# Gate-up products of two blocks as 84 rounds on the two halves of the TensorE array, followed by their eight sums and the steps of attention, with five PSUM banks in a ring

## The chip, the cores and the metric

The kernel runs on one core of one Trainium2 chip. A core has TensorE (PE in the profile, with its weight loads as PEld), VectorE (DVE), ScalarE (ACT), GpSimd (POOL) and SyncE (SP, which here only starts DMAs). The metric is the device time of one execution in microseconds.

## The reference

Input `x` is 2048 tokens of 448 features. It is normalised, and the result feeds two branches whose sum is added to `x`.

```python
xn = _layernorm(x)
# branch A: 16 heads of 28, four segments of 512 tokens, one after the other
q, k, v = heads(xn @ wq), heads(xn @ wk), heads(xn @ wv)
p = softmax(q_s @ k_s.T * scale + causal_mask)          # within segment s
o = g * (phi(q_s) @ M) / (phi(q_s) @ z + 1e-6) + (1 - g) * (p @ v_s)
M, z = M + phi(k_s).T @ v_s, z + sum(phi(k_s))
A = o @ wo
# branch B: a gated unit, 1792 wide
B = (sigmoid(xn @ w_gate) * (xn @ w_up)) @ w_down
return x + A + B
```

## The kernel before

**Numbers.** A wide product is made of fp32r parts: each operand is a high part plus a low part, and high·high, high·low and low·high are summed in PSUM. The 448 features lie in four chunks of the 128 partitions. Three chunks are full; chunk 3 holds the last 64 features twice: rows 0 to 63 hold the high part of `xn`, rows 64 to 127 its low part, and the weights stand there twice. So a product over all features takes 3×3+2 = 11 instructions (`TERMS`, line 53). The last of them, `(3, 7)`, also adds low·low in rows 64 to 127. `xs[b]` holds `xn` transposed, seven chunks for each of four blocks `b` of 512 tokens; `wgu[f]` holds chunks 0 to 7 of the gate and up weights for 128 of the 1792 columns, `f` from 0 to 13.

**The gated branch** (`gated`, line 166) takes `f` in pairs (`f0`, step `FG` = 2) and within each pair the four blocks. A block has four outputs of 128×512 (gate and up for two `f`), each of 11 products into one bank `pgu` (line 247): 44 instructions. When both outputs of an `f` stand, line 255 takes a Tanh of the gate's (`sg`, ACT), line 256 multiplies by the up's (DVE), line 258 copies the high part of `hh` (ACT) and line 259 makes the low part (DVE). A block then has four sums `down` (line 168), one for 128 tokens each: six products of `hh` with `wdn` (line 173) and an addition into `acc` (DVE, line 174). Lines 180 to 203 load the weights by SP and split them on ACT and DVE (lines 85 and 86).

**Attention** (`Pair`, `Unit`, from line 583) works on 32 pairs of heads and segments. A pair's scores are five banks `st` (line 612); each is copied to `w` by ACT (lines 616, 619), masked by POOL (line 627), and reduced for maxima by DVE (lines 629, 633). `weights` (line 639) combines the maxima with DVE and POOL in turn (lines 643 to 653), spreads them (`mb`, line 656), and in three parts subtracts them (DVE, line 666) and takes the exponential (ACT, line 667). Two pairs make a unit, whose product with `v` is `pa` (line 687), and which DVE finishes (lines 690, 136, 693). `attention` (line 700) hands these out in steps, 234 in all.

**What sets the order.** PE and SP run in the order in which the code is written (`MANUAL`, line 55). The loop at line 788 takes one place of the gated branch after another (each `yield`) and issues attention's steps in proportion, about 0.44 of a step to a place. A block has 20 places: three after each output and two after each sum, a sum following each output. Over the main part, ACT, DVE and POOL are put in an order by a scheduler when the kernel is built, and each of them then runs its own list strictly in that order. PSUM has eight banks, in `banks`, line 113: `gu` 2, `p` 2, `pd` 1, and for attention `s` 2 (for `st`) and `m` 1 (for `pa`).

## Time and profile before

| | us |
|---|---|
| median of the two runs shown | 689.47 (689.45 and 689.49) |
| the profiled execution | 689.46 |
| its span | 687.7 |

Of the span, PE is busy 681.7 us, DVE 567.4, ACT 342.6 and POOL 151.3. In the views a group of instructions is given as line, engine, operation, output<-input, shapes and count, then busy time in us and mean ns of one, then the idle time of the engine just before them with what ended it. In a table of windows each engine's busy time stands with the number of instructions. An instruction's own duration includes latency that the next one overlaps, so the spacing of a run of equal instructions is shorter than the mean of one.

### The profile page before, as it was taken

Reading aid. Unit: us, or ns where it says so; the run is one execution under the profiler, and the core shown is the slowest. Engines: PE = TensorE matmul, PEld = TensorE weight load, DVE = VectorE, ACT = ScalarE, POOL = GpSimd, SP = SyncE. Lnnn points to the kernel's source line nnn. Section 1 sums busy time; section 2 is a strip of 40 time slices with the busy share of each in tenths; the row PEclk is TensorE's granted clock in tenths of the full one; section 3 lists DMA queues with packets and bytes.
Section 4 is the critical chain, followed back from the end, with each engine's and each line's share of the span. In section 5 each row is a group of like instructions: output and inputs, shape, how many; then the busy total and the mean of one; then the engine's idle time right before and its main releaser. Section 6 shows DMA issues by size and latency. Waiting matters only on the chain.

```text
span 687.7 us, 10438 instructions
## 1 busy us (share of the span) xinstructions
PE 681.7 (99%) x3594; PEld 566.6 (82%) x3594; DVE 567.4 (83%) x994; ACT 342.6 (50%) x563; POOL 151.3 (22%) x349
## 2 busy tenths in 40 slices
PE   8999999999999999999999999999999999999997
PEld 7898888778878787787878878787787878878897
DVE  6765795767788988998898989989898899889863
ACT  4837555343554555543655446454653565446320
POOL 3500020101223222232332222322322322222000
PEclk9999999999999999999999999999999999999999
DMA  7446556696233323243223252314333332423342
GB/s 267 181 150 238 198 214 242 249 330 174 71 94 92 80 86 86 56 128 112 56 64 107 57 141 56 109 47 116 82 94 77 96 71 64 95 79 95 95 153 106
DMA packets 45796, 84.37 MB, mean 123 GB/s; under 512 B 6320, under 2 KB 20400, under 8 KB 45232
## 3 DMA queue, kind: packets, MB, share of 16 engines
q1 hardware_dynamic: 42736, 76.37, 35.8%
q0 software_dynamic: 3008, 7.34, 4.9%
q8 instruction: 28, 0.46, 0.3%
q14 instruction: 24, 0.20, 0.1%
HBM read 51.05 MB, written 32.64 MB: 122 GB/s over the span
## 4 chain that ended last, share of the span: by engine, by line
PE 70%; DVE 14%; issue 9%; POOL 4%; DMA 1%; ACT 1%; SPq 0%; POOLq 0%; ACTq 0%
PE pgu L247 26%; PE pd L173 13%; PE pp L355 10%; PE po L771 5%; PE pv L335 5%; PE st L612 3%; PE pa L687 3%; DVE mx L629 3%; DVE w L666 2%; POOL w L627 2%; DVE acc L174 2%; PE pmm L383 2%; PE n L401 2%; DVE hh L259 1%; DVE mx L633 1%
## 5 line engine op out<-in xcount | busy, mean ns | idle before, releaser
L247 PE MATMUL pgu<-xs,wgu 128*128 128x512 f32 x1232 | 304.1, 394 | 0.0
L247 PEld LDWEIGHTS pgu<-xs,wgu 128*128 128x128 f32 x1232 | 228.2, 188 | 47.4 <-issue 2.2
L173 PE MATMUL pd<-wdn,hh 128*128 128x448 f32 x672 | 156.0, 367 | 0.0
L627 POOL TENSOR_SCALAR_AFFINE_SELECT w<-w 128x256 f32<-128x256 f32 (+1 forms) x160 | 81.2, 509 | 236.4 <-ACT w L616 183.6
L173 PEld LDWEIGHTS pd<-wdn,hh 128*128 128x128 f32 x672 | 122.5, 188 | 12.3 <-issue 0.6
L667 ACT ACTIVATE w<-w 128x1024 f32<-128x1024 f32 (+1 forms) x96 | 87.3, 915 | 65.0 <-DVE w L666 64.2
L666 DVE TENSOR_TENSOR w<-w,mb 128x1024 f32<-128x1024 f32 (+1 forms) x96 | 98.9, 1045 | 0.1
L616 ACT ACTIVATE w<-st 128x512 f32<-128x512 f32 x128 | 74.9, 590 | 45.3 <-PE st L612 44.9
L629 DVE TRANSPOSE_TENSOR_REDUCE mx<-w 128x32 f32<-128x1024 f32 x64 | 79.0, 1235 | 17.0 <-POOL w L627 17.0
L355 PE MATMUL pp<-xs,wqk 128*128 128x512 f32 x308 | 77.7, 401 | 0.0
L174 DVE TENSOR_TENSOR acc<-pd,acc 128x448 f32<-128x448 f32 x112 | 67.1, 599 | 1.2 <-PE pd L173 1.1
L355 PEld LDWEIGHTS pp<-xs,wqk 128*128 128x128 f32 x308 | 56.8, 188 | 13.4 <-issue 2.4
L258 ACT ACTIVATE hh<-sg 128x512 fp32r<-128x512 f32 x56 | 35.2, 628 | 56.4 <-DVE sg L256 49.3
L612 PE MATMUL st<-qk 84*128 84x128 f32 (+3 forms) x256 | 61.9, 312 | 0.0
L255 ACT ACTIVATE sg<-pgu 128x512 f32<-128x512 f32 x56 | 33.2, 594 | 49.4 <-PE pgu L247 49.2
L612 PEld LDWEIGHTS st<-qk 84*128 84x128 f32 x256 | 47.6, 189 | 6.9 <-ACT w L616 0.3
L656 DVE STREAM_TRANSPOSE mb<-top 128x1024 f32<-128x1024 f32 x32 | 39.8, 1242 | 10.5 <-POOL top L653 10.1
L362 DVE TENSOR_TENSOR qk<-pp,qk 128x512 fp32r<-128x512 f32 x28 | 19.3, 688 | 29.8 <-ACT e L360 23.7
L259 DVE SCALAR_TENSOR_TENSOR hh<-sg,hh 128x512 fp32r<-128x512 f32 x56 | 38.7, 691 | 2.6 <-ACT hh L258 2.4
L335 PE MATMUL pv<-wv,xs 128*128 128x448 f32 x176 | 39.6, 376 | 0.4 <-DVE xs L102 0.3
L687 PE MATMUL pa<-w,vv 128*32 128x128 f32 (+3 forms) x512 | 39.7, 436 | 0.2
L256 DVE SCALAR_TENSOR_TENSOR sg<-sg,pgu 128x512 f32<-128x512 f32 x56 | 37.3, 665 | 1.8 <-PE pgu L247 1.6
(100 smaller groups left out, 640.6 us busy)
## 6 DMA issues: line engine op xcount, KB each, us to landing
qk<-qd SPq DMA_DIRECT2D x192, 112.0 KB
qd<-qk SPq DMA_DIRECT2D x28, 512.0 KB
raw<-in_w_ffn SPq DMA_DIRECT2D x14, 512.0 KB
vd<-vst SPq DMA_DIRECT2D x4, 1024.0 KB
vv<-vd SPq DMA_DIRECT2D x16, 256.0 KB
od<-w POOLq DMA_DIRECT2D x16, 256.0 KB, 3.8
sums<-od SPq DMA_DIRECT2D x32, 128.0 KB
out<-acc SPq DMA_DIRECT2D x16, 224.0 KB
```

The costliest lines, as they stand in the source:

```text
L173: T.matmul(pd[:, :D], l, r, start=n == 0, stop=n == len(mms) - 1)
L174: V.tensor_add(acc[b][:, t, :], pd[:, :D], acc[b][:, t, :])
L247: T.matmul(dst, wgu[f][:, w, side * P:(side + 1) * P], xs[b][:, a, :], start=n == 0, stop=n == len(TERMS) - 1)
L335: T.matmul(pv[:, :D], xs[b][:, a, t * P:(t + 1) * P], wv[w], start=n == 0, stop=n == len(TERMS) - 1)
L355: T.matmul(pp, wqk[c][:, w, :], xs[b][:, a, :], start=n == 0, stop=n == len(TERMS) - 1)
L612: T.matmul(st[:, at:at + L - kb * P], self.qk[:KS, 1, h, kb * P:(kb + 1) * P], self.qk[:KS, 0, h, kb * P:], start=True, stop=True)
L616: A.activation(w, st, AF.Copy)
L627: G.affine_select(d, d, pattern=pattern, base=0, channel_multiplier=-1, compare_op=ALU.is_ge, fill=MASK)
L629: V.tensor_reduce(mx[:, 16 * (n - 1):16 * (n + 1)], w3[:, n // 2, :2 * L].rearrange("p (b n) -> p b n", n=32), axis=mybir.AxisListType.X, ...
L666: V.tensor_sub(w, w, m)
L667: A.activation(w, w, AF.Exp, scale=SCALE)
L687: T.matmul(pa[32 * j:32 * j + 32, kb * P:], self.vv[:, kb, 32 * j:32 * j + 32], self.pairs[j // 2].block(j % 2, kb), start=kb == 0, stop=k ...
```

## The change

A block's 44 products of 128 rows become 42 *rounds*. A round is two products of 64 rows that stand next to each other, one on rows 0 to 63 of the array, the other on rows 64 to 127, into two different banks: the gate's and the up's of one `f`. `PHASES` lists four phases of a block, the first and second `f` with the halves one way round (11 rounds each), then both again turned (10 rounds each), so that each bank gets both halves of every term. The term that was `(3, 7)` is now taken over the 64 rows of the high part alone, once for each output; `xd` is a second copy of that part in the other half of the partitions (made by POOL, once for each block), and which half of chunk 3 holds the low part now depends on `b`.

The four phases of a block have no places in them, so no step of attention is issued there. After the first two phases stands one *mark* each: ACT copies a single element of `xs[b]` onto itself, chunk 6 after the first phase, chunk 5 after the second. It can run when the phase's products with that chunk are done, and later products with that chunk wait for it. These are the tenth round of the second phase (the 42nd of the block's 84 instructions, then the third phase) and, for the second mark, the tenth round of the third phase (the 63rd instruction, then the fourth phase).

Two blocks (`WINDOW`) run one after the other in this way, 84 rounds; then come their eight sums, each now followed by five places, and attention's steps among them. The five banks `gu`, `p`, `gu`, `p`, `pd` are taken in turn for outputs and sums. `raw`, into which the gate-up weights are loaded, has one buffer instead of two. The very first block keeps its 128-row products (`whole`).

```diff
+WINDOW = 2
+PHASES = ([None, (3, 3), (0, 0), (0, 4), (4, 0), (1, 1), (1, 5), (5, 1), (2, 2), (2, 6), (6, 2)],
...
+          [(5, 1), (1, 1), (1, 5), (0, 0), (0, 4), (4, 0), (3, 3), (2, 2), (2, 6), (6, 2)])
...
+    def high_tail(b, side):
+        r = slice(64 * side, 64 * side + 64)
+        return xs[b][r, 3, :] if side == b % 2 else xd[b // 2][r, :]
...
+        def place(n):
+            return ("gu", "p", "gu", "p", "pd")[(ring[0] + n) % 5]
...
-            pd = bank("pd", tag)
+            pd = bank("pd", tag or place(0))
...
-            yield
-            yield
+            for _ in range(places):
+                yield
...
-            raw_up[f] = mid.tile([P, 1024], F32, name="raw", bufs=2)
+            raw_up[f] = mid.tile([P, 1024], F32, name="raw", bufs=1)
...
+        def halves(f0, b, ahead, hs):
+
+            pgu = {}
+            for k, terms in enumerate(PHASES):
+                f, turned = f0 + k % 2, k // 2
+                if not turned:
+                    pgu[f] = [opened(k) for _ in range(2)]
+                for n, term in enumerate(terms):
+                    for h in (1, 0) if turned else (0, 1):
+                        side, r = h ^ turned, slice(64 * h, 64 * h + 64)
+                        a, w = term or (3, 7)
+                        T.matmul(pgu[f][side], wgu[f][r, w, side * P:(side + 1) * P],
+                                 xs[b][r, a, :] if term else high_tail(b, side),
+                                 start=n == 0 and not turned, stop=n == len(terms) - 1 and bool(turned))
+                if not turned:
+
+                    mark = xs[b][64:65, 6 - k, 0:1]
+                    A.activation(mark, mark.bitcast(F32), AF.Copy)
+                else:
+                    hs.append(finish(pgu[f], f))
...
+            ahead[0, 2] = lambda: load_up(f0 + 2)
+            ahead[1, 3] = lambda: load_up(f0 + 3)
...
+                    halves(f0, b, ahead, hs)
+                pending.append(downs(f0, b, hs))
+                if f0 + b > 0 and (b + 1) % WINDOW == 0:
+                    while len(pending) > (1 if WINDOW == 1 or f0 + FG == NF and b == NB - 1 else 0):
+                        for part in pending.pop(0):
+                            yield from part
...
+            high = slice(64, P) if b % 2 else slice(0, 64)
+            G.tensor_copy(xd[b // 2][low_rows(b), :], xs[b][high, 3, :])
```

**PE**, from where the gated branch leaves the first block (`xs_65`) for the second (`xs_66`). Before:

```order
L247 MATMUL pgu<-xs_66,wgu 128x512 x22
L612 MATMUL st<-qk_1642 128x512
L247 MATMUL pgu<-xs_66,wgu 128x512 x11
L612 MATMUL st<-qk_1642 128x384
L612 MATMUL st<-qk_1642 128x128
L173 MATMUL pd<-wdn,hh 128x448 x6
L612 MATMUL st<-qk_1642 128x512
L247 MATMUL pgu<-xs_66,wgu 128x512 x11
L173 MATMUL pd<-wdn,hh 128x448 x6
```

Now, where line 277 is the half-row product, line 193 the sum and line 671 the score:

```order
L277 MATMUL pgu<-xd_73,wgu 128x512
L277 MATMUL pgu<-xs_66,wgu 128x512 x21
L277 MATMUL pgu<-xd_73,wgu 128x512
L277 MATMUL pgu<-xs_66,wgu 128x512 x61
L193 MATMUL pd<-wdn,hh 128x448 x18
L671 MATMUL st<-qk_1645 128x512
L193 MATMUL pd<-wdn,hh 128x448 x6
L671 MATMUL st<-qk_1645 128x384
L671 MATMUL st<-qk_1645 128x128
L193 MATMUL pd<-wdn,hh 128x448 x6
```

Outputs, sums and scores alternated; now all 84 half-row products of this block stand together and the scores come among the sums behind them.

**ACT**, in the third block of the second pair of `f`. Before, with line 667 the exponential, 255 the Tanh, 258 the copy to `hh`, and 616 and 619 the copies of scores:

```order
L255 ACTIVATE sg<-pgu 128x512
L616 ACTIVATE w<-st 128x512
L667 ACTIVATE w<-w 128x2x512
L667 ACTIVATE w<-w 128x2x2x256
L667 ACTIVATE w<-w 128x2x2x128
L258 ACTIVATE hh<-sg 128x512
L616 ACTIVATE w<-st 128x512
L619 ACTIVATE w<-st 128x2x256
L255 ACTIVATE sg<-pgu 128x512
```

Now, with line 283 the mark, 726 the exponential, 236 the Tanh, 239 the copy to `hh`, 675 the copy of a score and 100 a split of weights:

```order
L675 ACTIVATE w<-st 128x512 x3
L283 ACTIVATE xs_67<-xs_67 1x1
L726 ACTIVATE w<-w 128x2x512
L726 ACTIVATE w<-w 128x2x2x256
L726 ACTIVATE w<-w 128x2x2x128
L100 ACTIVATE wdn<-rawd 128x448
L283 ACTIVATE xs_67<-xs_67 1x1
L236 ACTIVATE sg<-pgu 128x512
L239 ACTIVATE hh<-sg 128x512
L236 ACTIVATE sg<-pgu 128x512
L239 ACTIVATE hh<-sg 128x512
```

The three exponentials of a pair of heads lay between two Tanhs; now they lie ahead of the second mark, and none is left between the Tanhs.

**DVE**, at the same place. Before, with line 256 the product for `sg`, 259 the low part of `hh`, 174 the addition of a sum, 649, 651 and 656 steps of the maxima, 629 a reduction for maxima and 666 the subtraction:

```order
L256 SCALAR_TENSOR_TENSOR sg<-sg,pgu 128x512
L649 TENSOR_TENSOR mx<-mx,up 64x2x16
L651 TENSOR_TENSOR top<-mx,up 32x32
L174 TENSOR_TENSOR acc_69<-pd,acc_69 128x448
L259 SCALAR_TENSOR_TENSOR hh<-sg,hh 128x512
L656 STREAM_TRANSPOSE mb<-top 128x1024
L629 TENSOR_REDUCE mx<-w 128x32
L666 TENSOR_TENSOR w<-w,mb 128x2x512
L174 TENSOR_TENSOR acc_70<-pd,acc_70 128x448
L666 TENSOR_TENSOR w<-w,mb 128x2x2x256
L666 TENSOR_TENSOR w<-w,mb 128x2x2x128
L256 SCALAR_TENSOR_TENSOR sg<-sg,pgu 128x512
```

Now, from there into the fourth block, with line 725 the subtraction, 237 the product for `sg`, 240 the low part of `hh`, 101 a split and 194 the addition of a sum:

```order
L725 TENSOR_TENSOR w<-w,mb 128x2x2x128
L101 TENSOR_TENSOR wdn<-rawd,wdn 128x448
L237 SCALAR_TENSOR_TENSOR sg<-sg,pgu 128x512
L240 SCALAR_TENSOR_TENSOR hh<-sg,hh 128x512
L237 SCALAR_TENSOR_TENSOR sg<-sg,pgu 128x512
L240 SCALAR_TENSOR_TENSOR hh<-sg,hh 128x512
L237 SCALAR_TENSOR_TENSOR sg<-sg,pgu 128x512
L101 TENSOR_TENSOR wgu<-raw,wgu 128x1024
L240 SCALAR_TENSOR_TENSOR hh<-sg,hh 128x512
L237 SCALAR_TENSOR_TENSOR sg<-sg,pgu 128x512
L194 TENSOR_TENSOR acc_71<-pd,acc_71 128x448
L240 SCALAR_TENSOR_TENSOR hh<-sg,hh 128x512
```

DVE's list had attention's work between a block's four operations on outputs; now the eight operations of two blocks stand together, with only two splits and one addition among them.

More of the change, by code (lines that the diff above doesn't have):

```diff
@@ L82, with low_rows @@
     acc = [keep.tile([P, NT, D], F32, name=f"acc{b}") for b in range(NB)]
+    xd = [keep.tile([P, L], F32R, name=f"xd{n}") for n in range(NB // 2)]
+    def low_rows(b):
+        return slice(64, P) if b % 2 == 0 else slice(0, 64)
+    def high_tail(b, side):
+        r = slice(64 * side, 64 * side + 64)
+        return xs[b][r, 3, :] if side == b % 2 else xd[b // 2][r, :]
     def split(hi, lo, src):
@@ new lines, in opened, with whole @@
+        def opened(k):
+            tile = bank("pgu", place(0))
+            ring[0] += 1
+            return tile
+        def whole(f0, b, ahead, hs):
+            pgu = []
+            for k in range(2 * FG):
+                f, side = f0 + k // 2, k % 2
+                pgu.append(opened(k))
+                for n, (a, w) in enumerate(TERMS):
+                    T.matmul(pgu[k], wgu[f][:, w, side * P:(side + 1) * P], xs[b][:, a, :],
+                             start=n == 0, stop=n == len(TERMS) - 1)
+                    if n in (3, 7):
+                        yield
+                if side == 1:
+                    hs.append(finish(pgu[k - 1:], f))
+                yield
+                if (b, k) in ahead:
+                    ahead[b, k]()
@@ L216, in gated, with downs @@
+        def downs(f0, b, hs):
+            end = f0 + FG == NF and b == NB - 1
+            return [down(b, hs, wdn, t, ("pd", "s")[t % 2] if end else None, 2 if end or f0 + b == 0 else 5)
+                    for t in range(NT)]
+        pending = []
         for f0 in range(0, NF, FG):
@@ L268, in gated @@
-                end = f0 + FG == NF and b == NB - 1
-                todo += [down(b, hs, wdn, t, ("pd", "s" if end else "gu")[t % 2]) for t in range(NT)]
-        rest.extend(todo)
-    N_FFN = NF // FG * NB * 20 - 12
+                if f0 + b == 0:
+                    yield from whole(f0, b, ahead, hs)
+                else:
+                    halves(f0, b, ahead, hs)
[4 more added lines that the diff above has]
+                            yield from part
@@ L276 @@
+        rest.extend(pending.pop())
+    N_FFN = NF // FG * NB * 20 - 20
     with tc.tile_pool(name="front", bufs=2) as sb, tc.manual_schedule(engines=FRONT):
```

81 lines of the change are left out of this document (31 added, 50 removed), and 2 rows, old and new, of the table PHASES.

## The prediction

> **What bounds the kernel now.** The page comes first: busy shares, their course over 40 slices, and the engines on the chain that ended last.
>
> ```profile
> span 687.7 us, 10438 instructions
> PE 681.7 (99%) x3594; PEld 566.6 (82%) x3594; DVE 567.4 (83%) x994; ACT 342.6 (50%) x563; POOL 151.3 (22%) x349
> PE   8999999999999999999999999999999999999997
> DVE  6765795767788988998898989989898899889863
> ...
> PE 70%; DVE 14%; issue 9%; POOL 4%; DMA 1%; ACT 1%; SPq 0%; POOLq 0%; ACTq 0%
> ```
>
> PE is busy 99% of the span and in nearly every slice; DVE is at 8 to 9 tenths from the first third on; PE carries 70% of the chain, DVE 14%. The windows of the middle, with busy time and, after the engines, the granted clock, tell how near the second bound is:
>
> ```profile
> core 0: us, PE busy (x) PEld busy (x) DVE busy (x) ACT busy (x) POOL busy (x), PEclk, DMA share, GB/s
> 200.00:300.00 100.00, 99.86 (x551) 80.95 (x550) 90.88 (x149) 52.52 (x83) 27.77 (x66) 1.00 0.33 93
> ...
> 500.00:600.00 100.00, 100.00 (x535) 82.59 (x534) 89.57 (x144) 51.58 (x83) 26.82 (x65) 1.00 0.34 81
> sum 400.00, PE 399.79 PEld 326.58 DVE 359.89 ACT 209.68 POOL 108.86; mean PE 99.95 PEld 81.65 DVE 89.97 ACT 52.42 POOL 27.21
> ```
>
> In these 400 us PE never rests, and DVE works 89.97 of each 100 us. So PE bounds, with DVE one tenth behind. The timeline of PE gives the length of the stage that is changed (start, us, instructions merged):
>
> ```profile
> 157.68 5.60 PE L247 MATMUL pgu<-xs,wgu 128*128 128x512 f32 x24
> 163.12 0.40 PE L612 MATMUL st<-qk 84*128 84x512 f32 x1
> 163.35 2.67 PE L247 MATMUL pgu<-xs,wgu 128*128 128x512 f32 x11
> ```
>
> ```profile
> 635.37 2.68 PE L247 MATMUL pgu<-xs,wgu 128*128 128x512 f32 x11
> 637.89 1.37 PE L173 MATMUL pd<-wdn,hh 128*128 128x448 f32 x6
> ```
>
> Of the 24 products at 157.68 the last 22 are block 1's, so that block begins 2 products later, about 158.1 us. The last output ends at 637.89. Between lie 27 blocks: 479.8/27 = 17.8 us a block, **35.5 us for two**; DVE works 0.8997 of this, **31.9 us for two blocks**. The spacing of products comes from the first rows: 24 of them start between 157.68 and 163.12, (163.12−157.68)/24 = **0.227 us** for 512 columns.
>
> **What the change takes away.** Of 88 spacings for two blocks 84 remain if a round costs what a product costs: 4×0.227 = 0.9 us, and 27/2 times that 12.3 us in all. That needs two things that the trace of before can only bound.
>
> ```profile
> L687 PE MATMUL pa<-w,vv 128*32 128x512 f32 x128 | 17.0, 605 | 0.0
> L401 PE MATMUL n<-phi,mst 112*128 112x512 f32 x24 | 12.3, 591 | 0.0
> L383 PE MATMUL pmm<-vst,kn 128*112 128x128 f32 x96 | 11.9, 272 | 0.0
> L173 PE MATMUL pd<-wdn,hh 128*128 128x448 f32 x672 | 156.0, 367 | 0.0
> L247 PEld LDWEIGHTS pgu<-xs,wgu 128*128 128x128 f32 x1232 | 228.2, 188 | 47.4 <-issue 2.2 <-DVE qk L362 0.2 <-DVE mx L633 0.2
> ```
>
> A product on a 32-column strip of the array (line 687) takes 17.0/128 = 0.133 us of busy time, and a whole-array product with the same 512 columns and the same plain fp32 (line 401) 12.3/24 = 0.51: four strips run 3.9 abreast. Strips of columns are not halves of rows, but it is the nearest row, so I take the halves as abreast: a round 0.227. The other end is one after the other, 0.454. The second thing is weight loads: two a round instead of one. At line 383, with 112 columns loaded for each product, products follow at 11.9/96 = 0.124 us, so two loads take at most 0.248 a round if they take turns, 0.021 over what I use; if a load holds the path for its full mean of 0.188, two make 0.376. I take 0.227, as 0.248 is an upper bound drawn from short products, and keep 0.248 for the range. The end on the other side: the sum's six products of 448 columns at 637.89 follow at (1.37−0.367)/5 = 0.201, so 64 columns cost 0.026, 512 columns 0.21, and 0.016 is fixed; if the second half hides that, a round is 0.211. A change between whole-array and half-row products, twice a window, has no row; between 0 and the 0.272 of a short product's latency, I take 0 (double would be 7 us in all).
>
> **What the change moves.** PE's rounds hold no step of attention; the scores all come among the eight sums. With the rounds at 84×0.227 = 19.1 us and the 0.9 saved, PE by itself would need 34.6 us for two blocks, 15.5 of them for sums and scores. DVE has 31.9 us of work for the same, which fits only if it has work during the rounds too. Its list says otherwise: all of attention's operations come ahead of the first `sg` of the two blocks, and after that nothing but `sg`, `hh`, a split and an addition until the first reduction of the next scores. And the marks force the first part to be over early: ACT's list has the exponentials ahead of a mark, and PE can't pass the tenth round of the second phase without the first mark, nor the tenth of the third without the second. Queued behind the waiting PE are all later rounds, and behind them Tanh, `sg` and the sums. In the order as built, in 6 of the 13 windows of two blocks the last exponentials stand ahead of the first mark and in 7 ahead of the second (in two of those one or more exponentials come behind it).
>
> ```profile
> L256 DVE SCALAR_TENSOR_TENSOR sg<-sg,pgu 128x512 f32<-128x512 f32 x56 | 37.3, 665 | 1.8 <-PE pgu L247 1.6 <-ACT w L667 0.2
> L259 DVE SCALAR_TENSOR_TENSOR hh<-sg,hh 128x512 fp32r<-128x512 f32 x56 | 38.7, 691 | 2.6 <-ACT hh L258 2.4
> L174 DVE TENSOR_TENSOR acc<-pd,acc 128x448 f32<-128x448 f32 x112 | 67.1, 599 | 1.2 <-PE pd L173 1.1
> L86 DVE TENSOR_TENSOR wgu<-raw,wgu 128x1024 fp32r<-128x1024 f32 x14 | 17.2, 1226 | 0.3 <-ACT wgu L85 0.3
> L629 DVE TRANSPOSE_TENSOR_REDUCE mx<-w 128x32 f32<-128x1024 f32 x64 | 79.0, 1235 | 17.0 <-POOL w L627 17.0
> L656 DVE STREAM_TRANSPOSE mb<-top 128x1024 f32<-128x1024 f32 x32 | 39.8, 1242 | 10.5 <-POOL top L653 10.1
> L649 DVE TENSOR_TENSOR mx<-mx,up 64x32 f32<-64x32 f32 x32 | 5.7, 178 | 8.1 <-POOL up L648 8.0
> L651 DVE TENSOR_TENSOR top<-mx,up 32x32 f32<-32x32 f32 x32 | 5.6, 174 | 6.7 <-POOL up L650 6.2
> ```
>
> ```profile
> L255 ACT ACTIVATE sg<-pgu 128x512 f32<-128x512 f32 x56 | 33.2, 594 | 49.4 <-PE pgu L247 49.2
> L258 ACT ACTIVATE hh<-sg 128x512 fp32r<-128x512 f32 x56 | 35.2, 628 | 56.4 <-DVE sg L256 49.3 <-PE pd L173 4.7 <-DVE mx L645 2.3
> L616 ACT ACTIVATE w<-st 128x512 f32<-128x512 f32 x128 | 74.9, 590 | 45.3 <-PE st L612 44.9
> L667 ACT ACTIVATE w<-w 128x512 f32<-128x512 f32 x32 | 20.0, 624 | 2.2 <-DVE w L666 2.0
> L627 POOL TENSOR_SCALAR_AFFINE_SELECT w<-w 128x256 f32<-128x256 f32 x96 | 53.9, 562 | 168.8 <-ACT w L616 117.7 <-ACT w L619 49.7
> ```
>
> So one window is a circle of five pieces:
> 1. From the round that needs the mark to the end of the 84. The second mark holds instruction 63 of 168: 53 rounds, 12.0 us. The first holds instruction 42: 63.5 rounds, 14.4 us.
> 2. From the last round to DVE's first reduction: Tanh 0.594, `sg` 0.665, copy to `hh` 0.628, two copies of scores 2×0.590 (behind it in ACT's list), the mask 0.562: 3.6 us.
> 3. DVE's remaining work. In pieces 1 and 2 it can do only four `sg` (2.7), four `hh` (2.8), one addition (0.6) and the split (1.2), 7.3 us. Left of 31.9: 24.6 us.
> 4. Its idle time inside that: the maxima pass between DVE and POOL, and DVE stood idle 17.0+10.5+8.1+6.7 = 42.3 us for that before, 1.3 for each of 32 pairs; 2.5 pairs a window (32 over 13) make 3.3. Ends: 0 and double.
> 5. The last exponential, 0.624, and the mark; one element has no row, between 0 and the 0.59 of a score's copy, I take 0.3: 0.9 us.
>
> Sum: 44.4 us with the second mark, 46.8 with the first; (7×44.4+6×46.8)/13 = 45.5. That is above PE's own 34.6, so DVE's circle decides, and a window costs 45.5−35.5 = **10.0 us more** than now. The last window hands half of its sums, and of attention's steps, to the output stage: 12.5 windows, 125 us. The block alone at the start has hardly any attention and is counted at nothing.
>
> **Edits at nothing.** Five banks in a ring: the second block's first output waits for the Tanh of the first (0.594, ten rounds or 2.3 us after), the third for `sg` (21 rounds): hidden while ACT and DVE are free, and after the marks they are. `xd`: four copies by POOL in the front, of 512 elements a row where the mask's 256 take 0.562, so 1.1 us each, on an engine busy 22% of the span. One buffer for `raw`: load and split lie a block (42 rounds, 9.5 us) apart; SP waits with attention's loads behind it if a split is late, but those are issued two pairs ahead. Cover gone, a split that comes 1 us late holds the Tanh behind it in ACT's list once a window, 13 us in all. Attention's own loads and the DMAs from POOL move with their steps and keep their order.
>
> The sum stands against the profiled execution's own 689.46 us (the median is 689.47): 689.5+125 = 814.5, **815 us**.
>
> **Rivals.**
>
> *DVE keeps pace.* PE stays the bound and only the four spacings show: 689.5−12.3 = 677. For it: DVE has 3 us of slack in 35.5, and PE never waited before. It decides the matter if DVE's idle time in a window stays under 34.6−31.9 = 2.7 us; against it, pieces 1 and 2 hold 15.6 us and only 7.3 of work. With 0.211 a round it gains 27×42×0.016 = 18 more, 659. Chance 0.12, of which 0.05 beats the kernel before by over 2%.
>
> *The marks are never late.* If a pair's weights are done before the rounds begin, only piece 2 is lost from PE's stream: 34.6+3.6 = 38.2, 2.7 more than now, 12.5×2.7 = 34, 723 us. For it: ACT is busy only half of the time. Chance 0.13.
>
> *The clock drops.* PE waits in every window.
>
> ```profile
> core 0: us, PE busy (x) PEld busy (x) DVE busy (x) ACT busy (x) POOL busy (x), PEclk, DMA share, GB/s
> 683.00:685.00 2.00, 1.16 (x6) 0.75 (x4) 0.62 (x1) 0.00 (x0) 0.00 (x0) 1.00 0.31 115
> 685.00:687.70 2.70, 0.00 (x0) 0.00 (x0) 0.00 (x0) 0.00 (x0) 0.00 (x0) 0.71 0.23 85
> ```
>
> ```profile
> L442 PE MATMUL warm<-ident 128*128 128x128 f32 x20 | 4.6, 429 | 1.5 <-POOL ident masks.py:199 1.5
> L445 PE MATMUL warm<-ident 128*128 128x128 f32 x10 | 1.3, 275 | 0.0
> ```
>
> The last product ends 1.16 us into the first of these windows, near 684.2, and in the last 2.7 us the granted clock means 0.71: full for 1.1 us and half for the rest, so it fell 2 us after PE stopped. At the start, products on the cold array take 0.429 instead of 0.275, over 4.6 us of work. If each window has a wait of that kind at the mark, 4.6 us of rounds at half pace lose 2.3 us: 815+12.5×2.3 = 844. Chance 0.15. The Trainium skill ("TensorE: Matmul & The Clock Gate", HAM oscillation) says that a gap of over about 3.4 us brings the half clock; the trace agrees as to the direction, with 2 us in the one case that it shows.
>
> *The loads take turns.* At 0.376 a round, pieces 1 grow by (7×53+6×63.5)/13 = 57.8 rounds of 0.149, 8.6 us; 815+12.5×8.6 = 923. Chance 0.04, for all that lies between one round and two. The Trainium skill (same page, Part 3, measured speedup) gives four row tiles as 3.07 times one, not 4; by that a round would be 0.227×4/3.07 = 0.296 and the sum 815+12.5×57.8×0.069 = 865, an estimate from that page, which no row here shows.
>
> *The halves don't run abreast,* so the change doesn't do what it says: 0.454 a round, 57.8×0.227 = 13.1 us a window, 979 us. Against it, the strips. Chance 0.04.
>
> **How the numbers follow.** The forecast, DVE's circle, has 0.52. Its own bounds: without piece 4 and with 0.211 a round the window is 45.5−3.3−0.9 = 41.3, 762 us; with piece 4 doubled and 0.248 it is 45.5+3.3+1.2 = 50.0, 871 us. The range takes in the marks never late (723) and the dropped clock (844): 720 to 870. It leaves out the faster case (0.12), the loads (0.04) and the halves one by one (0.04), 0.20 together. A measurement of this kernel tells about 2% from no change, 675.7 to 703.3 us. Faster by more: 0.05. Within: 0.07. Slower: 0.88.
>
> **What would show it.** Right: PE's share falls to about 83%; its idle time stands before line 277, ended by ACT line 283, and before the scores of line 671, ended by ACT; DVE's busy time stays near 567 us, and in windows of a few us it is nearly empty late in the 84 rounds and full among the sums; a window of two blocks is 42 to 50 us long; products of line 277 start in twos, and twos follow at 0.227. Wrong: twos at another spacing, PE above 95%, waits before line 277 ended by DVE's `acc` or by DMA, or a clock below 1.00 in most windows, which would move cost from DVE's circle to the array.

## The result, and the profile after

| | before | after |
|---|---|---|
| median of two runs, us | 689.47 | 839.54 (838.88 and 840.20) |
| span of the profiled execution, us | 687.7 | 838.5 |
| ratio, with its 95% interval | | 1.2175 (1.2155 to 1.2194) |

The page of the changed kernel, in the same parts as before's: busy time, the course over 40 slices with the granted clock, and the engines on the chain that ended last.

```profile
span 838.5 us, 12676 instructions
PE 731.2 (87%) x4674; PEld 583.2 (70%) x4674; DVE 575.7 (69%) x994; ACT 360.7 (43%) x617; POOL 137.1 (16%) x353
PE   8999999899779795979779895979779886979898
DVE  6657866754886769584965858585874959587663
PEclk9999999899899998989999897989898989899999
...
PE 46%; DVE 24%; issue 13%; ACT 7%; DMA 5%; POOL 4%; POOLq 0%; SPq 0%; ACTq 0%; DVEq 0%
```

DVE's busy time grew by 8 us only, yet its row now swings between 4 and 9 tenths where it had stood at 8 and 9, and PE's row swings against it. On the chain PE fell from 70% to 46%, and DVE rose from 14% to 24%. The windows of the middle, one by one and then their mean:

```profile
core 0: us, PE busy (x) PEld busy (x) DVE busy (x) ACT busy (x) POOL busy (x), PEclk, DMA share, GB/s
200.00:300.00 100.00, 84.81 (x602) 68.55 (x600) 68.21 (x107) 43.13 (x73) 17.21 (x47) 0.93 0.22 61
600.00:700.00 100.00, 82.60 (x568) 64.06 (x569) 71.23 (x111) 42.98 (x71) 17.29 (x49) 0.90 0.26 62
sum 500.00, PE 419.78 PEld 326.03 DVE 353.71 ACT 216.65 POOL 89.56; mean PE 83.96 PEld 65.21 DVE 70.74 ACT 43.33 POOL 17.91
```

Neither engine is full any more: PE 83.96 of 100 us (99.95 before), DVE 70.74 (89.97): two engines that both wait take turns. PE's busy time even rose, by 49.5 us over the whole span, though 42 rounds stand where 44 products stood: 27.7 us of it are the products of `pa`, which run at about half pace behind their waits (28 of them in 4.03 us in the window below, where a run of 32 without a wait takes 2.36).

```profile
L687 PE MATMUL pa<-w,vv 128*32 128x128 f32 (+3 forms) x512 | 39.7, 436 | 0.2
```

```profile
L746 PE MATMUL pa<-w,vv 128*32 128x256 f32 (+3 forms) x512 | 67.4, 574 | 51.1 <-ACT w L726 51.1
```

The first of these lines is of the kernel before, the second of the changed one. The waits of PE, in order of size (us in total, times, the longest), and then the groups of DVE and ACT with the longest idle time of that kind, below them the exponentials (line 667) of the kernel before:

```profile
PE pa L746 <- ACT w L726: 51.1, 12, 7.3
PE pgu L277 <- ACT xs L283: 25.2, 9, 6.1
PE st L671 <- ACT w L675: 16.0, 16, 3.8
PE pgu L277 <- DVE ts L459: 3.8, 1, 3.8
```

```profile
L726 ACT ACTIVATE w<-w 128x1024 f32<-128x1024 f32 (+1 forms) x96 | 85.7, 912 | 123.1 <-DVE w L725 121.4
L237 DVE SCALAR_TENSOR_TENSOR sg<-sg,pgu 128x512 f32<-128x512 f32 x56 | 38.4, 685 | 101.0 <-ACT sg L236 100.8
```

```profile
L667 ACT ACTIVATE w<-w 128x1024 f32<-128x1024 f32 (+1 forms) x96 | 87.3, 915 | 65.0 <-DVE w L666 64.2
```

PE waits for ACT's exponentials (line 726, at `pa`) and marks (line 283), ACT's exponentials wait 121.4 us (64.2 before) for DVE's subtractions, and DVE waits 100.8 us (its idle time there was 1.8 before) for the Tanh that PE's rounds must first allow: the circle is closed. One window of two blocks shows it turning, from the end of one run of 84 rounds to the end of the next, in the timelines of PE, DVE and ACT (start, us, instructions merged, idle time before):

```profile
391.09 7.41 PE L277 MATMUL pgu<-xs,wgu 64*128 64x512 f32 x62
...
413.24 4.03 PE L746 MATMUL pa<-w,vv 128*32 128x512 f32 x28 [5.21 <-ACT w L726]
...
429.71 2.78 PE L277 MATMUL pgu<-xs,wgu 64*128 64x512 f32 x21 [1.05 <-ACT xs L283]
436.92 4.60 PE L277 MATMUL pgu<-xs,wgu 64*128 64x512 f32 x23 [4.42 <-ACT xs L283]
...
443.63 7.18 PE L277 MATMUL pgu<-xs,wgu 64*128 64x512 f32 x61
```

```profile
396.91 0.69 DVE L237 SCALAR_TENSOR_TENSOR sg<-sg,pgu 128x512 f32<-128x512 f32 x1 [5.17 <-ACT sg L236]
...
402.11 1.25 DVE L688 TRANSPOSE_TENSOR_REDUCE mx<-w 128x32 f32<-128x1024 f32 x1 [0.30 <-POOL w L686]
```

```profile
428.84 0.60 ACT L675 ACTIVATE w<-st 128x512 f32<-128x512 f32 x1 [4.14 <-DMA od<-w]
...
433.93 2.71 ACT L726 ACTIVATE w<-w 128x1024 f32<-128x1024 f32 x3 [4.27 <-DVE w L725]
436.66 0.20 ACT L283 ACTIVATE xs<-xs 1x1 fp32r<-1x1 f32 x1
```

The rounds end at 391.09+7.41 = 398.50; DVE's first reduction starts at 402.11, the second mark at 436.66, and the next rounds end at 443.63+7.18 = 450.81: 52.3 us for a window that took 35.5. PE stops once at `pa` (5.21) and twice at a mark (1.05, 4.42). The second mark stands in ACT's list right behind three exponentials, which had waited 4.27 us for DVE. Ahead of that ACT stood 4.14 us because the copy of a score goes to a buffer `w` that the DMA of a finished unit (`od`) still read; by way of POOL, which masks these scores ahead of its next step of the maxima, DVE stood 2.79 us for it. DVE's busy time in these pieces:

```profile
402.11:436.66 34.55, 23.26 (x147) 16.45 (x146) 28.12 (x46) 14.13 (x21) 8.43 (x25) 0.95 0.37 94
436.66:450.66 14.00, 13.74 (x106) 11.27 (x106) 5.17 (x8) 5.70 (x11) 0.00 (x0) 0.88 0.12 39
```

Of the 34.55 us to the mark DVE works 28.12; of the next 14.00, when PE works 13.74, it works 5.17.

**Where the 150.8 us of span went.** Block 1 begins at 162.15 where it began at 158.1: +4.0 (the wait of 3.8 for `ts`). From there to the first sum behind the last round (780.90 in the timeline; behind the last output it was 637.89) it is 618.8 where it was 479.8: +139.0. The rest, from there to the end, is 57.6 where it was 49.8: +7.8. Inside the 618.8 stand the lone block and the rounds of the first window, 48.1 us for three blocks that took 53.3, a gain of 5.2, and 12 windows of 47.56 in the mean, each from the end of one run of rounds to the end of the next, 12.0 more each, 144.2 in all.

### The profile page after: what moved, and what is told of

It reads as the page before. It is cut to its first block, busy times and chain, and to the rows that moved or that the text cites. A ratio compares the mean times of both kernels' runs of the same rounds, so it can differ in the third digit from the quotient of the medians.

```text
span 838.5 us, 12676 instructions
## 1 busy us (share of the span) xinstructions
PE 731.2 (87%) x4674; PEld 583.2 (70%) x4674; DVE 575.7 (69%) x994; ACT 360.7 (43%) x617; POOL 137.1 (16%) x353
## 3 DMA queue, kind: packets, MB, share of 16 engines
q1 hardware_dynamic: 42736, 76.37, 29.8%
## 4 chain that ended last, share of the span: by engine, by line
PE 46%; DVE 24%; issue 13%; ACT 7%; DMA 5%; POOL 4%; POOLq 0%; SPq 0%; ACTq 0%; DVEq 0%
PE pgu L277 18%; PE pp L412 8%; DVE mx L688 6%; DVE w L725 5%; PE pa L746 5%; PE po L830 4%; PE pv L392 4%; ACT w L726 3%; DVE acc L194 3%; PE pd L193 3%; DVE mb L715 3%; DMA od<-w 3%; POOL w L686 2%; DVE mx L692 1%; ACT w L675 1%
## 5 line engine op out<-in xcount | busy, mean ns | idle before, releaser
L277 PE MATMUL pgu<-xs,wgu 64*128 64x512 f32 x2214 | 282.0, 405 | 27.1 <-ACT xs L283 25.2
L277 PEld LDWEIGHTS pgu<-xs,wgu 64*128 64x128 f32 x2214 | 229.3, 195 | 76.0 <-ACT xs L283 29.7
L193 PE MATMUL pd<-wdn,hh 128*128 128x448 f32 x672 | 159.8, 375 | 0.0
L726 ACT ACTIVATE w<-w 128x1024 f32<-128x1024 f32 (+1 forms) x96 | 85.7, 912 | 123.1 <-DVE w L725 121.4
L193 PEld LDWEIGHTS pd<-wdn,hh 128*128 128x128 f32 x672 | 124.2, 192 | 16.9 <-issue 7.7
L686 POOL TENSOR_SCALAR_AFFINE_SELECT w<-w 128x256 f32<-128x256 f32 (+1 forms) x160 | 70.9, 450 | 389.2 <-ACT w L675 335.5
L746 PE MATMUL pa<-w,vv 128*32 128x256 f32 (+3 forms) x512 | 67.4, 574 | 51.1 <-ACT w L726 51.1
L675 ACT ACTIVATE w<-st 128x512 f32<-128x512 f32 x128 | 73.0, 595 | 81.6 <-PE st L671 68.7
L237 DVE SCALAR_TENSOR_TENSOR sg<-sg,pgu 128x512 f32<-128x512 f32 x56 | 38.4, 685 | 101.0 <-ACT sg L236 100.8
L746 PEld LDWEIGHTS pa<-w,vv 128*32 128x32 f32 x512 | 22.0, 134 | 94.4 <-ACT w L726 73.7
L671 PEld LDWEIGHTS st<-qk 84*128 84x128 f32 x256 | 46.6, 193 | 29.8 <-ACT w L675 20.7
```

Source lines behind the costliest of these rows:

```text
L193: T.matmul(pd[:, :D], l, r, start=n == 0, stop=n == len(mms) - 1)
L277: T.matmul(pgu[f][side], wgu[f][r, w, side * P:(side + 1) * P], xs[b][r, a, :] if term else high_tail(b, side), start=n == 0 and not turne ...
L671: T.matmul(st[:, at:at + L - kb * P], self.qk[:KS, 1, h, kb * P:(kb + 1) * P], self.qk[:KS, 0, h, kb * P:], start=True, stop=True)
L675: A.activation(w, st, AF.Copy)
L686: G.affine_select(d, d, pattern=pattern, base=0, channel_multiplier=-1, compare_op=ALU.is_ge, fill=MASK)
L726: A.activation(w, w, AF.Exp, scale=SCALE)
```

## The experiments

Each run changes the order, the marks or the products alone, as far as they can be parted. All times are medians in us; a ratio is against the kernel before on the same chip.

**Whole products in the changed order.** The order of the groups, the ring and the single buffer stay; only `halves` is replaced, so that there are no rounds and no marks.

```diff
-                    halves(f0, b, ahead, hs)
+                    for _ in whole(f0, b, ahead, hs):
+                        pass
```

> The changed kernel with 128-row products in place of the half-row rounds, 88 for two blocks, no marks; the order of outputs, sums and attention stays as changed. If the bunched order is what costs (DVE empty during the outputs, its chain too long among the sums): 12 us more for four products in each of 13 windows, up to 31 us less for the waits before line 277 that end with the marks, so 805 to 840 us, DVE busy still near 70% and the waits before pa still there. If the half-row products and what they bring (marks, changes of form, weight loads) are what costs: 690 to 710 us.

Measured: 796.67 (one run). The waits of this kernel, and its windows of the middle:

```profile
PE pa L747 <- ACT w L727: 47.5, 11, 5.4
PE st L672 <- ACT w L676: 15.7, 15, 4.5
```

```profile
sum 500.00, PE 442.38 PEld 348.29 DVE 377.86 ACT 222.07 POOL 98.07; mean PE 88.48 PEld 69.66 DVE 75.57 ACT 44.41 POOL 19.61
```

So 107.2 of the 150.1 us need no half-row product and no mark, and the waits at `pa` and at the scores are nearly those of the changed kernel (47.5 and 15.7 against 51.1 and 16.0). The time lies a little below what was expected for the order.

**Places given back to the outputs.** The same kernel with three places after each output's parts and two after each sum; the eight sums of two blocks still stand together.

```diff
-                    for _ in whole(f0, b, ahead, hs):
-                        pass
+                    yield from whole(f0, b, ahead, hs)
...
-            return [down(..., 2 if end or f0 + b == 0 else 5)
+            return [down(..., 2)
```

> The changed kernel with 128-row products, no marks, and the places of a block put back into its outputs (three to an output, two to a sum); the eight sums of two blocks still stand together and the banks still go in a ring. If it is attention's absence from the outputs that costs: 690 to 715 us. If the ring of five banks, the bunched sums or the single raw buffer cost by themselves: 740 us or more, near the 797 us of the bunched run with whole products.

Measured: 700.93, ratio 1.016 (1.0143 to 1.0177). The same windows:

```profile
sum 500.00, PE 493.03 PEld 404.77 DVE 431.11 ACT 242.19 POOL 118.46; mean PE 98.61 PEld 80.95 DVE 86.22 ACT 48.44 POOL 23.69
```

PE is at 98.61 of 100 us again and DVE at 86.22. Only the places moved, and 95.7 us went: attention's absence from the outputs is the cost. Ring, single buffer and bunched sums together leave 11.5.

**Marks on whole products.** Both kernels with the two marks, after the first two outputs of a block.

```diff
+                if k < 2 and f0 + b > 0:
+                    mark = xs[b][64:65, 6 - k, 0:1]
+                    A.activation(mark, mark.bitcast(F32), AF.Copy)
```

> The bunched run with whole products (796.7 us) plus marks: after the first and second output of a block ACT copies one element of xs onto itself, chunk 6 and chunk 5, so that the second output's product with chunk 6 and the third's with chunk 5 wait for it. No half-row product is in it. If the marks behind ACT's exponentials explain what the halves cost on top of the bunched order: 820 to 850 us, with waits before line 256 ended by ACT. If the halves cost by their form: 797 to 803 us.

> The run with whole products and places in the outputs (700.9 us) plus the same marks. If marks explain most of the 81 us between it and the half-row rounds with places in the phases (781.6 us): 740 to 775 us. If changes of form do (19 us of them, less 12 for the rounds) and half clock behind them: 701 to 715 us.

Measured: 800.14, ratio 1.1603 (1.1569 to 1.1637), and 706.46, ratio 1.0245 (1.0215 to 1.0274): 3.5 and 5.5 us more. Marks alone are cheap in either order; that they explain what the half-row products cost beyond the order falls.

**Half-row products in the order of before.** Rounds and marks stay, outputs take turns in `gu` and `p`, each sum goes to `pd`, and every phase has three places and then one sum of the block before with its two places. The second kernel has DVE make the marks.

```diff
-                    pgu[f] = [opened(k) for _ in range(2)]
+                    pgu[f] = [bank("pgu", tag) for tag in ("gu", "p")]
...
+                for _ in range(3):
+                    yield
+                if todo:
+                    yield from todo.pop(0) or ()
```

> Half-row rounds and marks as changed, but with the places of the kernel before: three places and one sum of an earlier block after each phase, so that attention's steps and sums lie between the phases; outputs in gu and p, sums in pd. If the bunched order is what costs: back to the kernel before, less the four rounds a window, 677 us, plus what late marks cost, 675 to 705 us; PE busy over 95%, clock 1.00. If the half-row rounds themselves cost: 800 us or more, with waits before line 277.

> As the run before, but the marks are made by DVE instead of ACT. If late marks cost time in the spread order because ACT's list holds exponentials ahead of them, this differs from the run before by some us; if marks are never late there, both are the same within 3 us.

Measured: 790.81, ratio 1.1467 (1.1443 to 1.149), and 793.20, ratio 1.152 (1.1489 to 1.1552). A miss: the order theory wanted 675 to 705, its rival 800 or more. The waits of PE with ACT's marks:

```profile
PE pd L193 <- DVE acc L194: 43.5, 30, 4.2
PE st L671 <- ACT w L675: 6.0, 5, 2.9
PE pgu L277 <- ACT xs L283: 2.7, 3, 1.4
```

The waits at the marks are nearly gone; a new one stands before the sums, which share one bank and wait for DVE's addition. Whether ACT or DVE makes the marks makes no difference that these runs tell apart.

**The same with the ring.** Ring and bunched sums as in the changed kernel, four places after each phase and one after each sum.

```diff
+                for _ in range(4):
+                    yield
...
-            return [down(..., 2 if end or f0 + b == 0 else 5)
+            return [down(..., 2 if end or f0 + b == 0 else 1)
```

> The changed kernel with half-row rounds, marks and bunched sums, but four places after each phase and one after a sum. Two changes of form for each phase cost 108 x 0.18 = 19 us by the spacings of the spread run (0.315 for 0.226, 0.297 for 0.201), the rounds give 12 back. If attention's absence costs: 700 to 730 us. If the marks on ACT's list cost in every order, more: 740 to 800 us, with waits before line 277 ended by ACT.

Measured: 781.64, ratio 1.1335 (1.13 to 1.1371), a second miss of the order theory; the time lies where marks that cost in every order would put it, with 16.9 us of waits at marks, but on whole products in this order marks cost only 5.5. The wait before the sums fell to 7.0 us, and half-row products stay 80.7 us above whole ones with places in the outputs. So order is most of the cost in the changed kernel, and yet order alone does not make half-row products cheap.

**Marks on POOL,** in the changed kernel.

```diff
-                    A.activation(mark, mark.bitcast(F32), AF.Copy)
+                    G.tensor_copy(mark, mark)
```

> The changed kernel with the marks made by POOL, whose list holds no exponentials. If the marks are the place where DVE's circle closes: the waits before line 277 (31 us) go, and most of that shows, 810 to 822 us. If the circle only closes at another place (the scores and pa behind ACT's exponentials) the waits move there: 828 to 842 us.

Measured: 823.93 (one run), 15.6 less, between the two expectations. The waits of PE show the one for a mark about halved:

```profile
PE pa L746 <- ACT w L726: 50.4, 11, 7.3
PE st L671 <- ACT w L675: 16.2, 16, 3.9
PE pgu L277 <- POOL xs L283: 13.1, 6, 3.3
```

**Filling PE's wait.** 24 products that nothing uses go to `pa` ahead of its own, which overwrite them.

```diff
+            for _ in range(24):
+                T.matmul(pa[:, :P], ident, ident, start=True, stop=True)
```

> The changed kernel with 24 idle products of 128 columns (about 0.109 us for each of two passes, 5.2 us) ahead of each of the 16 pa groups, into pa's own bank; they add work that no result uses. If the half clock after long waits costs PE: pa's 28 products fall from 4.48 to about 2.4 us and the total falls by 10 to 30 us. If DVE's circle alone sets the end: no gain, 838 to 870 us.

Measured: 843.41 (one run). A window of 100 us of this kernel, then its waits:

```profile
200.00:300.00 100.00, 91.88 (x699) 77.35 (x698) 67.95 (x106) 42.67 (x74) 15.34 (x47) 0.98 0.22 61
```

```profile
PE pgu L277 <- ACT xs L283: 28.1, 13, 6.1
...
PE pa L748 <- ACT w L726: 4.2, 7, 0.6
```

```profile
L745 PE MATMUL pa<-ident 128*128 128x128 f32 x768 | 88.3, 275 | 0.0
L748 PE MATMUL pa<-w,vv 128*32 128x128 f32 (+3 forms) x512 | 46.8, 437 | 4.4 <-ACT w L726 4.2
```

The clock is back at 0.98 in this window (0.93 before the fill), over the whole run 0.982 for 0.937; the waits at `pa` are down from 51.1 to 4.2, and its products from 67.4 to 46.8. The time does not fall. So the slower clock is a consequence of the waits, and this fill wins nothing. It does not show that the slow clock costs nothing: the fill is itself 88.3 us of products where 46.9 of waits and 20.6 of slow pace went, and it leaves the waits at marks, 28.1 us, and the slow rounds behind them.

**A window of one block.**

```diff
-WINDOW = 2
+WINDOW = 1
```

> The changed kernel with WINDOW 1: one block's 42 rounds, then four sums of the block before. DVE's empty stretch is cut twice as often but is half as long, and Tanh to first reduction is paid twice: by the circle (2.5 or 4.9 us of rounds after the mark, 3.6, half of 24.6+3.3, 0.9 and half of what DVE does in the rounds taken off) 21 to 23.5 us a block, 780 to 830 us. If changes of form ruled it would be slower than the changed kernel by 27 x 0.18 = 5 us: 845.

Measured: 809.73 (one run). Half the length of the rounds wins 29.8 of 150 us; PE now waits 48.0 us at marks, 24 times, and 12.7 at `pa`. DVE's empty stretch is shorter, but there are twice as many; its idle time ahead of line 237 falls only from 100.8 to 81.8.

**Whole products in the changed kernel's phases.** A last pair of theories on what the half-row products themselves cost. In the changed kernel both pairs of a block finish late (after 32 and 42 of its 42 rounds; whole products finish the first after 22 of 44). These kernels do whole products in four phases, so that the first pair is finished after 34 of 44, with marks, in both orders.

```diff
-                f, side = f0 + k // 2, k % 2
-                pgu.append(opened(k))
...
+                f, turned = f0 + k % 2, k // 2
+                own, other = ((6, 2), (5, 1)) if k % 2 == 0 else ((5, 1), (6, 2))
+                if not turned:
+                    pgu[f] = [opened(k) for _ in range(2)]
+                    mms = [(1, t) for t in SAME + [(1, 1)]] + [(0, t) for t in SAME + [own]]
+                else:
+                    mms = [(1, t) for t in [own, (1, 5), other, (2, 2), (2, 6)]]
+                    mms += [(0, t) for t in [(1, 1), (1, 5), other, (2, 2), (2, 6)]]
```

> Whole 128-row products in the changed kernel's order of groups, with marks, but in its four phases too: part of gate and up of the first filter pair, part of the second's, the rest of the first's, the rest of the second's, so that the first pair's two sums are finished after 34 of 44 products of a block (after 32 of 42 rounds in the changed kernel, after 22 of 44 in the run of whole products with marks, 800.1 us). Theory: what the half-row products cost beyond the order (44 us) is that both pairs of a block finish late, so that ACT, whose list then has the marks and exponentials ahead of the first Tanh, and DVE with them have nothing to do of the FFN while the products run: about 835 to 850 us, products waiting some 20 to 30 us for marks, idle time of DVE ahead of its product of gate and up near 100 us. Rival: the half-row products themselves (their changes of form, their loads, their shorter cover) cost it: 795 to 810 us, as the run of whole products with marks, with its 3 us of waits for marks.

> The same four phases of whole products, with three of attention's places in each phase and two in each sum, as in the run of whole products with marks and places in the outputs (706.5 us); the run of half-row products with places in its phases took 781.6. Theory (late pairs): 765 to 785 us. Rival (the half-row products themselves): 700 to 715 us. Between 720 and 755 both have a share: changes of form and rounds are worth about 19 less 12 us, and what is left beside them would be the half-row products' own.

Measured: 806.40, ratio 1.1688 (1.1662 to 1.1714), and 721.69, ratio 1.0464 (1.0446 to 1.0481). Late pairs cost 6.3 us in the bunched order and 15.2 in the other; the theory that they are the rest falls, 721.69 lies at the lower edge of where both have a share, and 33.1 us stay with the half-row products. The waits of PE in the first of these:

```profile
PE pa L755 <- ACT w L735: 48.8, 10, 5.4
PE st L680 <- ACT w L684: 15.4, 15, 3.6
...
PE pgu L284 <- ACT xs L290: 2.9, 3, 1.3
```

Beside the changed kernel, `pa` and the scores wait as long; the difference is the marks, 2.9 against 25.2 us. The order of ACT's list tells what stands ahead of them. In the changed kernel (line, operation; the rows from the last score's copy to the first Tanh of a window):

```
L678 ACTIVATE w<-st 128x2x256
L726 ACTIVATE w<-w 128x2x512
L726 ACTIVATE w<-w 128x2x2x256
L726 ACTIVATE w<-w 128x2x2x128
L726 ACTIVATE w<-w 128x2x512
L726 ACTIVATE w<-w 128x2x2x256
L726 ACTIVATE w<-w 128x2x2x128
L283 ACTIVATE xs_65<-xs_65 1x1
L100 ACTIVATE wgu<-raw 128x1024
L100 ACTIVATE wdn<-rawd 128x448
L283 ACTIVATE xs_65<-xs_65 1x1
L236 ACTIVATE sg<-pgu 128x512
```

and the same place with whole products in phases:

```
L687 ACTIVATE w<-st 128x2x256
L735 ACTIVATE w<-w 128x2x512
L735 ACTIVATE w<-w 128x2x2x256
L735 ACTIVATE w<-w 128x2x2x128
L735 ACTIVATE w<-w 128x2x512
L290 ACTIVATE xs_65<-xs_65 1x1
L735 ACTIVATE w<-w 128x2x2x256
L735 ACTIVATE w<-w 128x2x2x128
L290 ACTIVATE xs_65<-xs_65 1x1
L100 ACTIVATE wgu<-raw 128x1024
L236 ACTIVATE sg<-pgu 128x512
```

Six exponentials ahead of the first mark there, four here and two more behind it. Over all windows, of 43 exponentials that stand behind a window's last score, 39 are ahead of the second mark in the changed kernel and 20 in the other. With the marks out of that list, on POOL, the changed kernel was 15.6 us faster (one run).

## Why the prediction was right, and where its sizes were off

**The cause** was named and holds: DVE is left without work during the rounds, PE waits for what DVE's work behind them releases, and the step of the change that does most of it is the move of attention's places out of the outputs (95.7 us between two kernels of whole products that differ in nothing but places). PE's share of the span fell to 87%, 84% in the middle, where 83% was given; its waits at marks and at scores, ended by ACT, and DVE's work, 575.7 us for 567.4, are as described. The rest of the cost, what the half-row products add, was not in the prediction.

**The pieces of the circle.** The boundaries shown above for one window (end of rounds, DVE's first operation of attention, end of the second mark, end of rounds), taken in the timelines of all 12 windows, give these means. In ten windows that first operation is a reduction of line 688; in two others DVE still had steps of an earlier pair in hand.

| piece | predicted | measured |
|---|---|---|
| 2: last round to DVE's first operation of attention | 3.6 | 3.6 (3.1 to 4.2) |
| 3: DVE's remaining work | 24.6 | 26.0 |
| 4 and 5: its idle time there, last exponential and mark | 4.2 | 4.0 |
| 1: mark to the end of the rounds | 13.1, the mean of 12.0 and 14.4 | 14.0, always from the second mark |
| window | 45.5 | 47.6 |

The size that was off most is DVE's work. Over a whole window it is 34.0 us, not 31.9: the forecast gave every window the mean of the middle of the kernel before, but the lone block and the first window's rounds hold only 23 us of DVE's work for three blocks, so more falls to each window that follows. That the window hangs on this work shows from window to window: the five with over 36 us of it took 49.5 to 54.3 us, the seven with 29 to 35 took 42.8 to 47.1.

Piece 1 is longer for two reasons. Rounds behind a wait run slowly at first: in the window shown the last 53 rounds took 450.66−436.92 = 13.7 us instead of 12.0, with a clock of 0.88, and over the 12 windows the slow rounds behind second marks took 10.5 us more than at 0.227. And in the five windows without a stall the mark was ready before PE needed it. The agreement of pieces 4 and 5 is in part luck: in two windows, the one shown among them, DVE stood 2.8 and 2.4 us behind score copies that waited for the DMA of `od`. ACT waited so six times, 11.7 us in all, and never in the kernel before; the prediction took these DMAs to keep their order and counted nothing. Four of the 12 windows are above the 42 to 50 us that were given as a sign (50.9 to 54.3), eight inside.

**Where it closes** was named only in part. The prediction had PE wait at the marks; the larger wait is at `pa` inside the sums, 51.1 us, for the exponentials of scores that were issued just ahead in the same group of sums. In five of the 12 windows the rounds ran without any stall, in 19.2 to 19.7 us, and each time PE had stood 4.5 to 7.3 us at `pa` just before. For the length of the window it is the same circle, as the traces read: either wait ends with an exponential that waits for DVE.

**The sum.** 12.5 windows of 10.0 were forecast, 125 us; the span grew by 150.8. Twelve windows of 12.0 more make 144.2: 24 of the 25.8 us that the forecast lacks. Of the 12.0, 10.0 are DVE's idle time (13.6 us a window, as forecast, where it was 3.6) and some 2 the work that was mis-sized. What is left, −5.2 at the lone block and the first rounds, +7.8 behind the last round and +4.0 at the start of block 1, makes +6.6, where half a window and nothing else had been counted, 5.0; that they come so near is luck, as the start was not foreseen. (637.89, which the prediction calls the end of the last output, is the start of the sum behind it, 0.16 us earlier than that end; the sum doesn't change by it.) The chain at the start shows the load of `raw`, which now has one buffer, between DVE's operations:

```profile
148.82 5.55 DMA raw<-in_w_ffn
154.45 1.07 ACT wgu L100
...
162.15 4.21 PE pgu L277 x16
```

That the single buffer makes block 1 late is read from this chain and was not tried by itself. **The round** was taken right: by the trace's start times products start in twos, most often 3 to 4 ns apart and nearly all within 50, and the twos follow at 0.227 (966 of 1120 spacings lie between 0.210 and 0.235 us); a run of 84 without a stall takes 19.2 to 19.7. So the rivals of loads in turn (0.376 a round) and of halves one after the other (0.454) fall, and with them the estimate of 0.296 from the Trainium skill ("TensorE: Matmul & The Clock Gate", Part 3, measured speedup), which is for four row tiles; for two this trace shows 0.227. **The change of form** was taken as 0 and costs 0.09 us: from the start of the last half-row product to the start of a sum's product 0.315 (median of 14) against 0.227 for whole products (also of 14) in the kernel of whole products in the same phases. Twice a window that is some 2 us in all. Where each phase has places behind it, in the half-row kernel of 781.64 us, the trace has 198 changes; 18 of them, to and from `pa`, follow as they do with whole products, and the other 180 make some 16 us, a little less than the 19 that was expected.

**DVE keeps pace and marks never late** fall with the waits. **The dropped clock** came true as a sign: the middle's windows have 0.90 to 0.93. The prediction said that this would move the cost to the array. Little of it did: the rounds behind second marks lost 10.5 us in 12 windows, where the rival had 2.3 for each window, 29 us. What the slow products of `pa` cost is open, since with PE kept busy through the waits at `pa` the clock came back and the time didn't change, but the fill had a price of its own. The rule of the Trainium skill that was cited ("TensorE: Matmul & The Clock Gate", HAM oscillation) agrees with the trace as to the direction; most of the time doesn't hang on it here.

**The whole account,** from run to run: 689.5 before; 700.9 with ring, single buffer and bunched sums (+11.5); 796.7 without places in the outputs (+95.7); 800.1 with marks (+3.5); 806.4 with pairs that finish late (+6.3); 839.5 with rounds for whole products (+33.1). Three of these times are of one or two runs, so the small steps are sure to some 2 us only.

**What stays open.** Set against the last 33.1 us, 15.6 went when the marks left ACT's list, and the rows of that list show exponentials ahead of the marks that stand behind them with whole products. Why the lists are built otherwise was not tried: it would fit that the scheduler counts the two products of a round one after the other and so believes that attention has more time, but no run had the same list for both kinds of product. The other 17.5 us are not settled either: the change of form is some 2 of them, and DVE's idle time ahead of line 237 is 100.8 us in the changed kernel and 78.9 with whole products in phases, so most of them look like waits and not like products; this is argued, not shown. In the order with places, half-row and whole products differ by 59.9 us (781.6 and 721.7), with places at different points, so this pair is no single step. There some 20 us more of waits on PE (40.7 against 20.0, from the same view), 16 for changes of form and, as an estimate, 12 for the clock (0.974 against 0.993 of some 640 us), less 12 for the rounds saved, make 36; the rest is open.

## What to carry to other kernels

Where two engines are both over 80% busy, count for each stretch of the bounding engine's order what the other can do in it: a stretch without work for the second engine is added to the time at every turn, less the slack that this engine had (here 13.6 us of idle time less 3.6 in a window of 47.6), and shortening the first engine's own work (here 12 us in all) doesn't pay for it. Count the second engine's work turn by turn and not as a mean over the stage. If such work is to be bunched, as much of it must be in hand when the bunch begins as the second engine can do meanwhile (which no run here tried). A fence that has an engine run a tiny instruction is as late as whatever stands ahead of it in that engine's list, so where the list is made by a scheduler, look there before the price of the instruction.

## What the hardware showed beside that

- Two products of 64 rows on the two halves of the array, 512 columns, both with their own weight load, run fully abreast: 0.229 us a round with everything, against 0.227 for one whole product.
- Going from half-row to whole-array products, or back, costs about 0.09 us each way: 0.315 against 0.227 into a sum, and into half-row products 0.151 against 0.061 behind a score of 128 columns (medians of 31 and 40). Into `pa`, whose products use strips of 32 columns, it costs nothing more than from whole products: 0.315 against 0.318.
- After a wait of some microseconds rounds follow at 0.40 to 0.50 us for a few microseconds (71 of 1120 spacings), while the granted clock is lower; where such waits were filled with products ahead of `pa`, the mean clock rose from 0.937 to 0.982 and the time did not fall.
